# Attention in front of two expert mixtures, one core: tail scores cut into two parts of 288 keys, one exponential, one scaling and two casts placed elsewhere, and another order of work at the end of attention

## The chip, the cores and the metric

One core of a Trainium2 chip runs the whole program in one launch. The metric is the device time of a run in microseconds; 1092.76 us is the median of three runs of the kernel before. TensorE (PE in the rows, PEld its weight loads), VectorE (DVE), ScalarE (ACT), GpSimd (POOL) and SyncE (SP, which issues the transfers here) each work through their own list of instructions in order and wait for each other by semaphores.

## The reference

Sizes: 4 batches, 8 heads, 576 positions, 64 per head; both mixtures have 2304 tokens of 512, 8 experts and 1024 hidden units.

```python
scores = where(causal, -1e9, (q @ k.T) / sqrt(64))      # 576 x 576 for each batch and head
a      = exp(scores - scores.max(-1)); a /= a.sum(-1) + 1e-9
local  = a @ v
mem    = (phi(q) @ M_prev) / (phi(q) @ z_prev + 1e-6)   # phi(x) = elu(x) + 1
x      = g * mem + (1 - g) * local                      # g = sigmoid(beta), by head
# first mixture, soft slots: logits = x @ phi; d = softmax over all tokens; slot_in = d.T @ x
#   two layers per expert on its 4 slots; c = softmax over slots; x = c @ slot_out
# second mixture: P = exp(x @ w_gate - max), 8 rounds of row and column balancing
#   out = sum_e P[:, e] * (relu(x @ w1[e]) @ w2[e])
```

## The kernel before

Attention goes by pairs of heads: 16 pairs, four for each batch. A pair has five steps of queries: steps 0 to 3 are 128 queries each, for both heads, with 128 to 512 keys (in the rows a step is known by its width: step 2 has 384 keys, step 3 has 512); step 4 is the tail, the last 64 queries of both heads on 128 partitions with all 576 keys. A step goes through these stations, and the names are those of the rows:

- `scores`: TensorE multiplies into a PSUM bank `ps` (L385 and L386; the tail L366 and L371, in a bank of 512 keys and one of 64). VectorE negates, scales, masks and takes each row's minimum in one instruction, from `ps` to `sm` (L387, the tail L377 into `smt`); each is followed by a short read of the minimum, `mn`. ScalarE makes the exponentials in place with their sums (L394, `exp`).
- `transposes`: TensorE turns the 128x128 blocks of `sm` into `pt` (L437, the tail L419 and L425), ScalarE or VectorE copies them to `pA` (steps 0 and 1) or `pB` (L62, L66).
- `attend`: once a pair, values times probabilities into `po` (L476), copied to `ot` by ScalarE.
- The steps `post_...` of a pair run during the next pair: `post_r` makes the scale `r` from the sums (L522 to L532), `post_x` turns `ot` back into `px` (L541) and scales it (L544), `post_add` adds the memory part `x` on GpSimd, `post_t` turns `x` into `xT` (L566, copied by L66), `post_logits` multiplies by the slot weights into `pl` (L579, L585) and adds to `lt` (L592).
- The steps `pre_...` prepare a pair two ahead: each of `q` and `k` is split into a rounded part (`qh`, `kh`, and for the tail `qz`, `qx`) and a rest (by GpSimd, L268). `qx` is two copies of 64x64 by ScalarE. `pre_phi` makes phi(q) on VectorE (L336).

After each batch the pair that follows carries the routing of that batch (`route_turn` to `route_slots`: `plt`, `dd`, `pu`, `uacc`), spread over its steps and those of the pair behind it, so two pairs of each of the last three batches have more to do. After the last pair nothing runs beside its post and route steps; then `slot_inputs` (`psl`, `sT`) opens the first mixture, whose first layer is `ph` (L890).

The order of ScalarE and SyncE within attention is the order of the code; TensorE, VectorE and GpSimd get theirs from a scheduler, save where `tc.keep_in_program_order` pins an instruction. The code's order is `scores` of the next step, `attend`, `transposes`, with the steps in between hung at places by a table (`POS`, `at`). `LATE` puts an exponential off: `(2, 1): 1` says that the exponentials of step 2, second head, are issued behind the transposes of step 1, and so behind the copy of `pA`.

Weights of the first mixture come in 32 pieces of 1 MB (`wm`, L99). 14 have room of their own and are loaded during attention; 8 use memory that attention frees at its end; 10 use the memory of the first pieces again and wait until `ph` has read those. Behind them in SyncE's list stand the first weights of the second mixture (`raw`, `w`).

Of the kernel before, what the change touches and what calls it, by code (L numbers as in the profile page):

```python
# [21 lines left out]
def infini_attention_soft_moe_sinkhorn_moe(  # L22
# [22 lines left out]
    P = 128  # L45
# [66 lines left out]
    with ExitStack() as actx:  # L112
# [18 lines left out]
        nc.vector.memset(zero, 0.0)  # L131
        maskt = e2.tile([P, TAIL], BF16, name="maskt")
        nc.gpsimd.memset(maskt, 0.0)
        for j in range(2):
            sl = maskt[64 * j : 64 * j + 64]
            nc.gpsimd.affine_select(
                out=sl, in_=sl, compare_op=ALU.is_ge,
                fill=-BIG, base=0, pattern=[[-1, TAIL]], channel_multiplier=1,
            )
# [150 lines left out]
        def pre_qz(X):  # L290
            n = 4 * P
            qz, qx = X.qt = qtail[X.p % QTB]
            i = nc.vector.tensor_copy(
                qz.rearrange("p (a w) -> p a w", a=3)[:, 0::2], X.qd[:, :, n:]
            )
            if X.p > 1:
                tc.keep_in_program_order(i)
            for h in range(2):
                sl, cl = slice(D * h, D * h + D), slice(TAIL * h, TAIL * h + TAIL)
                copy(CFG["e_qx"], qx[sl, cl], X.qd[sl, h, n:])  # L300
            for h in range(2):
# [43 lines left out]

        LATE = {(0, 0): 4, (0, 1): 4, (1, 1): 0, (2, 1): 1, (3, 0): 2, (3, 1): 2}

# [6 lines left out]
        def scores(X, i):  # L354
            last = i == NT - 1
            n = P * (i + 1) if not last else S
            for h in range(1 if last else 2):
                sm = smt if last else e2.tile([P, 4 * P], F32, tag="sm", name="sm", bufs=SMB)
                mnc = X.mn[:, i, h : h + 1]
                if last:  # L360
                    parts = ((0, 4 * P), (4 * P, S))
                    pss = [pst("ps") for _ in range(2)]
# [11 lines left out]
                    mn2 = X.mn[:, NT, 0:1]  # L374
                    for c, msk in ((0, zero.to_broadcast([P, 4 * P])), (1, maskt)):
                        c0, c1 = parts[c]
                        nc.vector.tensor_tensor_reduce(  # L377
                            out=sm[:, c0:c1], in0=pss[c][:, 0 : c1 - c0], in1=msk, scale=QS,
                            scalar=mn2 if c else 3.0e38, op0=ALU.add, op1=ALU.min,
                            accum_out=mnc if c else mn2,  # L380
                        )
# [81 lines left out]
        def attend(X, i):  # L463
# [4 lines left out]
            for n, w, o0 in ((2, 2 * P, 0), (NT, W2, 2 * P)):  # L468
                po = pst("po")
                for j in range(n):  # L470

                    c0 = P * j if n == 2 else P * max(0, j - 2)
                    for h in range(2):
# [60 lines left out]
        def post_x(X, parts):  # L534
            x1 = X.ot.rearrange("p (t c) -> p t c", t=NT)
            end = X.p == NP - 1
            for t0, t1 in parts:
                px = pst("px")
                nt = t1 - t0
                for t in range(t0, t1):  # L540
                    nc.tensor.transpose(  # L541
                        px[:, P * (t - t0) : P * (t - t0) + P], X.ot[:, P * t : P * t + P], ident
                    )
                nc.vector.tensor_tensor(  # L544
                    out=x1[:, t0:t1].rearrange("p t (h d) -> p (t h) d", h=2),
# [4 lines left out]
                )  # L550
                if end:
                    nc.vector.tensor_add(X.x[:, t0:t1], X.x[:, t0:t1], x1[:, t0:t1])

# [21 lines left out]
        def post_logits(X):  # L575

            pl = pst("pl")
            for t in range(4):
                nc.tensor.matmul(  # L579
                    pl[32 * t : 32 * t + 32, 0:P], phi_sb[:, X.hp],  # L580
                    X.xT[:, P * t : P * t + P], start=True, stop=True,
                )

            for t in range(4):
                nc.tensor.matmul(  # L585
                    pl[32 * t : 32 * t + 32, P : P + TAIL], phi_sb[:, X.hp],
                    X.xT[:, 4 * P : S], start=True, stop=True,
                )
            if X.hp == 0:
                nc.vector.tensor_copy(lt, pl[:, 0 : P + TAIL])  # L590
            else:
                nc.vector.tensor_tensor(  # L592
                    out=lt, in0=lt, in1=pl[:, 0 : P + TAIL], op=ALU.add
                )

        def route_logits(b):
            m5 = e4.tile([P, 1], F32, tag="m5", name="m5")
            nc.vector.tensor_reduce(out=m5, in_=lt, op=ALU.max, axis=AX.X)
            R.m5 = m5

# [75 lines left out]
        def route_slots(b):  # L676
# [7 lines left out]
            for r in range(NHP + 1):  # L684
                for g in range(4):
# [35 lines left out]
        def at(p, n, f, *args):  # L721
# [12 lines left out]
        ROUTE = (  # L734
            ("ra", route_logits), ("rb", route_turn), ("rc", route_max), ("rd", route_factor),
            ("re", route_slots),
        )
        for p in range(NP):
# [18 lines left out]
            for n, (nm, f, *a) in enumerate(MEM):  # L757
                at(p, POS[nm] if p + 1 < NP else POS["mz"] + 2 * n, f, pairs[p], *a)
            if hp == NHP - 1 and p + 1 < NP:
# [4 lines left out]
            else:  # L764
                for n, f, *a in (
                    (1, post_r), (2, post_x, ((0, 2),)), (3, post_t, ((0, 2),)),
                    (3, post_x, ((2, 5),)), (3, post_t, ((2, 5),)), (9, post_logits),
                ):
                    at(p + 1, n, f, pairs[p], *a)
# [960 lines left out]
```

## Time and profile before

| what | value |
|---|---|
| median of three runs | 1092.76 us (1092.0 to 1095.72) |
| the profiled execution | 1093.55 us, its span 1091.8 us |
| TensorE busy over the span | 1058.1 us, 97% |
| VectorE, ScalarE, GpSimd busy | 790.7, 623.0, 730.1 us |
| attention with its end | from 0 to 254.75 us |
| first mixture | 254.75 to about 294 us |
| second mixture | the rest, where the page has TensorE at 9 tenths in all slices |

A busy share is that of an engine's instructions in the span. A wait is given in square brackets or behind the releaser. The granted clock of TensorE is 1.00 for 2.4 GHz and 0.50 for 1.2 GHz.

### The profile page before, as it was taken

To read this page: it belongs to the slowest core of one execution; us is meant where nothing else is said; L and a number is where in the kernel's file an instruction comes from. 1 tells how busy PE (TensorE), PEld (TensorE's weight loads), DVE (VectorE), ACT (ScalarE), POOL (GpSimd) and SP (SyncE) were. 2 spreads that over 40 slices of the span, in tenths; PEclk is the share of its full clock that TensorE was granted. 3 is DMA by queue.
4 is the path that set the end of the run, shared out by engine and by line. 5 is a ranking of instruction groups with operands and counts; after the bars stand their busy time and mean duration, and the time that the engine had idled before them with its cause. 6 is when DMAs were issued, how large, how long until landed. Compare 5 with 4: busy or idle time off the path is not lost.

```text
span 1091.8 us, 24586 instructions
## 1 busy us (share of the span) xinstructions
PE 1058.1 (97%) x9157; PEld 968.1 (89%) x9157; DVE 790.7 (72%) x1764; ACT 623.0 (57%) x1322; POOL 730.1 (67%) x683
## 2 busy tenths in 40 slices
PE   6999999988999999999999999999999999999998
PEld 4878878764477899999999999999999999999998
DVE  7888878764157466777777777777777777877776
ACT  7998989841243666456445645554564464456442
POOL 6655646400153499679678867968886796889765
PEclk9999999997989999999999999999999999999999
DMA  9476767568812014113210421321042132110211
GB/s 212 135 216 188 215 202 217 155 235 356 351 55 87 1 20 159 36 20 118 65 24 11 156 39 21 114 67 24 12 155 40 21 113 65 24 16 15 69 54 59
DMA packets 103574, 113.08 MB, mean 104 GB/s; under 512 B 69152, under 2 KB 79520, under 8 KB 99360
## 3 DMA queue, kind: packets, MB, share of 16 engines
q1 hardware_dynamic: 103024, 111.42, 33.8%
q8 instruction: 73, 1.20, 0.5%
q14 instruction: 45, 0.37, 0.1%
q10 hardware_dynamic: 432, 0.09, 0.0%
HBM read 95.74 MB, written 4.72 MB: 92 GB/s over the span
## 4 chain that ended last, share of the span: by engine, by line
PE 80%; DVE 5%; DMA 5%; ACT 4%; issue 3%; POOL 3%; SPq 0%; DVEq 0%; ACTq 0%; POOLq 0%
PE y L1530 56%; PE l L1146 5%; PE po L476 3%; PE pt L437 2%; PE y L1493 2%; DMA kd<-in_k_dram 2%; ACT sm L394 2%; PE pa L1093 2%; DMA wm<-in_moe_w_dram 2%; DMA w<-in_moe_w_dram 1%; PE ph L890 1%; PE ps L371 1%; PE ps L366 1%; DVE sm L387 1%; PE pt L419 1%
## 5 line engine op out<-in xcount | busy, mean ns | idle before, releaser
L1170 DVE SCALAR_TENSOR_TENSOR f<-l,f 128x512 f32<-128x512 f32 x268 | 183.8, 686 | 83.9 <-ACT a11h L1176 70.1
L1187 POOL TENSOR_TENSOR s1l<-f,s1h 128x512 fp32r<-128x512 f32 x67 | 87.3, 1303 | 116.6 <-ACT s1h L1176 116.6
L1544 DVE TENSOR_TENSOR accA<-accA,y 128x512 f32<-128x512 f32 x125 | 85.6, 685 | 54.0 <-PE y L1530 54.0
L1166 ACT ACTIVATE f<-l 128x512 f32<-128x512 f32 x67 | 40.1, 598 | 120.1 <-PE l L1146 119.5
L1176 ACT ACTIVATE a12h<-l 128x512 fp32r<-128x512 f32 x72 | 43.3, 601 | 103.0 <-PE y L1530 83.0
L1187 POOL TENSOR_TENSOR s4l<-f,s4h 128x512 fp32r<-128x512 f32 x67 | 87.7, 1308 | 17.3 <-PE y L1530 17.3
L1544 DVE TENSOR_TENSOR accB<-accB,y 128x512 f32<-128x512 f32 x125 | 85.7, 685 | 4.2
L1187 POOL TENSOR_TENSOR s2l<-f,s2h 128x512 fp32r<-128x512 f32 x67 | 87.6, 1307 | 1.3 <-ACT s2h L1176 0.5
L1187 POOL TENSOR_TENSOR s3l<-f,s3h 128x512 fp32r<-128x512 f32 x67 | 87.8, 1311 | 0.0
L1146 PE MATMUL l<-c4T,a 128*128 128x256 f32 x576 | 78.1, 278 | 0.0
L394 ACT ACTIVATE sm<-sm,mn 128x128 f32<-128x128 f32 (+3 forms) x128 | 70.9, 557 | 8.3 <-DVE mn L387 7.9
L1530 PE MATMUL y<-T2h,s2h 128*128 128x256 f32 x268 | 74.7, 279 | 0.0
L1530 PE MATMUL y<-T2l,s2h 128*128 128x256 f32 x268 | 74.1, 276 | 0.0
L1530 PE MATMUL y<-T2h,s2l 128*128 128x256 f32 x268 | 74.1, 276 | 0.0
L1530 PE MATMUL y<-T1h,s1h 128*128 128x256 f32 x268 | 74.0, 276 | 0.0
L1530 PE MATMUL y<-T1l,s1h 128*128 128x256 f32 x268 | 74.0, 276 | 0.0
L1530 PE MATMUL y<-T1h,s1l 128*128 128x256 f32 x268 | 74.0, 276 | 0.0
L1530 PE MATMUL y<-T4h,a22h 128*128 128x256 f32 x268 | 74.0, 276 | 0.0
L1530 PE MATMUL y<-T4l,a22h 128*128 128x256 f32 x268 | 74.0, 276 | 0.0
L1530 PE MATMUL y<-T4h,a22l 128*128 128x256 f32 x268 | 74.0, 276 | 0.0
L1530 PE MATMUL y<-BB1h,s3l 128*128 128x256 f32 x268 | 73.1, 276 | 0.9 <-POOL s3l L1187 0.9
L1530 PE MATMUL y<-BB2h,a12h 128*128 128x256 f32 x268 | 73.6, 279 | 0.0
(324 smaller groups left out, 4063.1 us busy)
## 6 DMA issues: line engine op xcount, KB each, us to landing
wm<-in_moe_w_dram SPq DMA_DIRECT2D x32, 1024.0 KB, 7.2
raw<-in_moe_w_dram SPq DMA_DIRECT2D x32, 512.0 KB, 3.6
w<-in_moe_w_dram SPq DMA_DIRECT2D x32, 512.0 KB, 5.4
qd<-in_q_dram SPq DMA_DIRECT2D x30, 288.0 KB, 4.2
kd<-in_k_dram SPq DMA_DIRECT2D x30, 288.0 KB, 4.3
c4T<-ct SPq DMA_DIRECT2D x224, 32.0 KB, 2.0
qp<-in_q_dram SPq DMA_DIRECT2D x15, 288.0 KB, 3.0
vt<-in_v_dram SPq DMA_DIRECT2D x16, 256.0 KB, 4.5
```

What stands on the lines that cost most here:

```text
L394: nc.scalar.activation(out=sm[:, 0:n], in_=sm[:, 0:n], func=AF.Exp, scale=-1.0, bias=mnc, accum_out=X.sums[:, i, h : h + 1],)
L437: nc.tensor.transpose(pt[:, o_ : o_ + P], pr[:, P * j : P * j + P], ident)
L476: nc.tensor.matmul(po[64 * h : 64 * h + 64, c0:w], X.vt[:, j, h, :], rhs, start=(j == 0), stop=(j == n - 1),)
L1093: nc.tensor.matmul(pa[32 * j : 32 * j + 32, 0:256], soT[:, c, :], w1[j][:, c, :], start=(c == 0), stop=(c == KD - 1),)
L1146: nc.tensor.matmul(ph[:, f, :], a4s[e][:, P * (KH * j + f) : P * (KH * j + f) + P], c4T[:, UT * u : UT * u + UT], start=True, stop=True,)
L1166: nc.scalar.activation(out=f_tile(g, nm), in_=ph(g, nm), func=AF.Relu)
L1170: nc.vector.scalar_tensor_tensor(out=f_tile(g, nm), in0=ph(g, src), scalar=0.0, in1=b, op0=ALU.max, op1=op)
L1176: nc.scalar.activation(out=h_tile(g, nm, "h"), in_=ph(g, nm) if a else FU[g, nm], func=AF.Relu if a else AF.Copy)
L1187: nc.gpsimd.tensor_tensor(out=lo, in0=FU[g, nm], in1=hi, op=ALU.subtract)
L1493: nc.tensor.matmul(Y[g, i], X[g, f"a{i}{j}", "hhl"[n]][:, f, :], BB[j, "hlh"[n]][:, f].rearrange("p a c -> p (a c)"), start=j == 1 and f = ...
L1530: nc.tensor.matmul(o_, a[:, f, :], b[:, f, :], start=n == 0, stop=n == 3 * KH - 1)
L1544: nc.vector.tensor_tensor(out=acc, in0=acc, in1=y, op=ALU.add)
```

## The change

1. The tail's scores go into two banks of 288 keys in place of 512 and 64. The mask tile `maskt` grows from 64 to 288 columns.
2. `(2, 1)` leaves `LATE`: both exponentials of step 2 are issued together, ahead of the copy of `pA`.
3. The scaling of `ot` (`post_x`, the part of four blocks) is kept in program order, which is behind the minima of step 2.
4. The two copies to `qx` go from ScalarE to GpSimd, from the third pair on.
5. The end of the last pair is written anew: `post_r` ahead of `attend`; `end_x`, `end_t` and `end_l` in place of `post_x`, `post_t` and `post_logits`, block by block, where one VectorE instruction for each block and head (64 columns) scales and adds; the first two blocks are turned back while `attend` still runs; copies to `xT` by ScalarE; the last sum of the logits and their maximum in one instruction, in the last pair of each batch; the sums of the weights in `route_slots` ahead of most `pu` in the last batch; the memory steps of the last pair earlier by one to three places.

```diff
-        maskt = e2.tile([P, TAIL], BF16, name="maskt")
+        SH = S // 2
+        maskt = e2.tile([P, SH], BF16, name="maskt")
...
-                copy(CFG["e_qx"], qx[sl, cl], X.qd[sl, h, n:])
+                copy("P" if X.p > 1 else CFG["e_qx"], qx[sl, cl], X.qd[sl, h, n:])
...
-        LATE = {(0, 0): 4, (0, 1): 4, (1, 1): 0, (2, 1): 1, (3, 0): 2, (3, 1): 2}
+        LATE = {(0, 0): 4, (0, 1): 4, (1, 1): 0, (3, 0): 2, (3, 1): 2}
...
-                    parts = ((0, 4 * P), (4 * P, S))
+                    parts = ((0, SH), (SH, S))
...
-                    for c, msk in ((0, zero.to_broadcast([P, 4 * P])), (1, maskt)):
+                    for c, msk in ((0, zero.to_broadcast([P, SH])), (1, maskt)):
...
+                    if n == NT and j == 2 and X.p == NP - 1:
+                        end_x(X, 0, 2)
...
+        def end_x(X, t0, t1):
+            px = pst("px")
+            for t in range(t0, t1):
+                nc.tensor.transpose(
+                    px[:, P * (t - t0) : P * (t - t0) + P], X.ot[:, P * t : P * t + P], ident
+                )
+            for t in range(t0, t1):
+                for h in range(2):
+                    c0 = P * (t - t0) + D * h
+                    xs = X.x[:, t, D * h : D * h + D]
+                    nc.vector.scalar_tensor_tensor(
+                        out=xs, in0=px[:, c0 : c0 + D], scalar=X.r2[:, t, h : h + 1], in1=xs,
+                        op0=ALU.mult, op1=ALU.add,
+                    )
+
+        def end_t(X, t0, t1):
...
+            px = pst("pxT")
+            for t in range(t0, t1):
+                nc.tensor.transpose(px[:, P * (t - t0) : P * (t - t0) + P], X.x[:, t], ident)
+            a, z = P * t0, min(P * t1, S)
+            copy("A", X.xT[:, a:z], px[:, 0 : z - a])
+
+        def end_l(X, t0, t1):
...
-                nc.vector.tensor_tensor(
+                i = nc.vector.tensor_tensor(
                     out=x1[:, t0:t1].rearrange("p t (h d) -> p (t h) d", h=2),
...
-                if end:
-                    nc.vector.tensor_add(X.x[:, t0:t1], X.x[:, t0:t1], x1[:, t0:t1])
+                if t0 == 0:
+                    tc.keep_in_program_order(i)
...
+            elif X.hp == NHP - 1:
+                R.m5 = e4.tile([P, 1], F32, tag="m5", name="m5")
+                nc.vector.tensor_tensor_reduce(
+                    out=lt, in0=lt, in1=pl[:, 0 : P + TAIL], scale=1.0, scalar=-3.0e38,
+                    op0=ALU.add, op1=ALU.max, accum_out=R.m5,
+                )
...
-        def route_logits(b):
-            m5 = e4.tile([P, 1], F32, tag="m5", name="m5")
-            nc.vector.tensor_reduce(out=m5, in_=lt, op=ALU.max, axis=AX.X)
-            R.m5 = m5
...
-                if r == 3:
+                if r == (0 if b == B - 1 else 3):
                     weight_sums(b)
...
-                at(p, POS[nm] if p + 1 < NP else POS["mz"] + 2 * n, f, pairs[p], *a)
+                at(p, POS[nm] if p + 1 < NP else (11, 13, 14, 14)[n], f, pairs[p], *a)
...
-                    (1, post_r), (2, post_x, ((0, 2),)), (3, post_t, ((0, 2),)),
-                    (3, post_x, ((2, 5),)), (3, post_t, ((2, 5),)), (9, post_logits),
+                    (0, post_r), (1, end_t, 0, 2), (1, end_x, 2, 5), (2, end_l, 0, 2),
+                    (2, end_t, 2, 4), (2, end_t, 4, 5), (3, end_l, 2, 4), (3, end_l, 4, 5),
+                    (9, post_logits),
```

The order on VectorE in an ordinary pair, from the scale `r` to the minima of step 3, before:

```order
L387 ISA sm,mn<-ps,maskw 128x384
L387 ISA mn 128x1
L532 RECIPROCAL r_858<-r_858 128x10
L544 TENSOR_TENSOR ot<-px,r_858 128x512
L387 ISA sm,mn<-ps,maskw 128x384
L387 ISA mn 128x1
L544 TENSOR_TENSOR ot<-px,r_858 128x128
L387 ISA sm,mn<-ps,maskw 128x512
```

and in the change:

```order
L388 ISA sm,mn<-ps,maskw 128x384
L388 ISA mn 128x1
L574 RECIPROCAL r_858<-r_858 128x10
L585 TENSOR_TENSOR ot<-px,r_858 128x128
L388 ISA sm,mn<-ps,maskw 128x384
L388 ISA mn 128x1
L585 TENSOR_TENSOR ot<-px,r_858 128x512
L388 ISA sm,mn<-ps,maskw 128x512
```

The scalings of 512 and of 128 columns have changed places, so the small one, not the large one, now stands between the two minima of step 2. ScalarE at the same place of a pair, before:

```order
L394 ACTIVATE sm,sums<-sm,mn 128x256
L394 ACTIVATE sm,sums<-sm,mn 128x384
L62 ACTIVATE pA<-pt 128x2x256
L394 ACTIVATE sm,sums<-sm,mn 128x384
L62 ACTIVATE pB<-pt 128x3x128
L394 ACTIVATE sm,sums<-sm,mn 128x512 x2
L62 ACTIVATE pB<-pt 128x3x128
L62 ACTIVATE qh<-qd 128x1024
L394 ACTIVATE smt,sums<-smt,mn 128x576
L62 ACTIVATE qx_148<-qd 64x64 x2
L62 ACTIVATE kh<-kd 128x1152
```

and in the change:

```order
L395 ACTIVATE sm,sums<-sm,mn 128x256
L395 ACTIVATE sm,sums<-sm,mn 128x384 x2
L62 ACTIVATE pA<-pt 128x2x256
L62 ACTIVATE pB<-pt 128x3x128
L395 ACTIVATE sm,sums<-sm,mn 128x512 x2
L62 ACTIVATE pB<-pt 128x3x128
L62 ACTIVATE qh<-qd 128x1024
L395 ACTIVATE smt,sums<-smt,mn 128x576
L62 ACTIVATE kh<-kd 128x1152
```

The copy of `pA` has gone behind the second exponential of step 2, and the two copies to `qx` have left the list. TensorE at the end of the last pair, from the end of `attend` to the turning of the logits, before:

```order
L476 MATMUL po<-pB,vt 64x64 x2
L522 MATMUL pz<-sums,ident 64x1
L541 MATMUL px<-ident,ot 128x128 x2
L566 MATMUL pxT<-ident,x 128x128 x2
L541 MATMUL px<-ident,ot 128x128 x3
L566 MATMUL pxT<-ident,x 128x128 x3
L579 MATMUL pl<-xT,phi_sb 32x128 x4
L585 MATMUL pl<-xT,phi_sb 32x64 x4
L604 MATMUL plt<-ident,lt 128x128
```

and in the change:

```order
L477 MATMUL po<-pB,vt 64x64 x2
L507 MATMUL pxT<-ident,x 128x128
L489 MATMUL px<-ident,ot 128x128 x2
L507 MATMUL pxT<-ident,x 128x128
L489 MATMUL px<-ident,ot 128x128
L514 MATMUL pl<-xT,phi_sb 32x128 x2
L507 MATMUL pxT<-ident,x 128x128 x3
L514 MATMUL pl<-xT,phi_sb 32x128 x2
L520 MATMUL pl<-xT,phi_sb 32x64 x4
L637 MATMUL plt<-ident,lt 128x128
```

The scale's `pz` and the first two `px` now stand ahead of these rows, among those of `po`.

## Rows read from the trace of the kernel before

**Rows 1.** Windows: us; busy of PE, PEld, DVE, ACT, POOL; granted clock; DMA share; GB/s.

```profile
100.97:114.25 13.28, 12.86 (x119) 10.92 (x116) 10.94 (x41) 12.32 (x33) 7.88 (x10) 1.00 0.59 182
127.55:142.83 15.28, 14.32 (x124) 11.56 (x122) 12.19 (x49) 12.77 (x36) 7.89 (x10) 1.00 0.77 225
142.83:158.12 15.29, 14.41 (x166) 12.15 (x167) 12.03 (x44) 12.53 (x34) 7.88 (x10) 1.00 0.60 179
```

**Rows 2.** Timeline of a pair: start, us, engine, instruction, [idle before <-releaser].

```profile
113.00 0.69 DVE L544 TENSOR_TENSOR ot<-px,r 128x512 f32<-128x512 f32 x1
...
113.60 0.55 DVE L387 CUSTOM_DVE_ANT_0 sm<-ps,maskw 128x384 f32<-128x384 f32 x1
...
114.08 0.28 DVE L544 TENSOR_TENSOR ot<-px,r 128x128 f32<-128x128 f32 x1
114.25 0.61 ACT L394 ACTIVATE sm<-sm,mn 128x384 f32<-128x384 f32 x1 [0.29 <-DVE mn L387]
114.28 0.68 DVE L387 CUSTOM_DVE_ANT_0 sm<-ps,maskw 128x512 f32<-128x512 f32 x1
...
115.01 0.55 PE L437 MATMUL pt<-ident,sm 128*128 128x128 f32 x3 [0.51 <-ACT sm L394]
...
118.04 0.71 POOL L268 TENSOR_TENSOR qz<-qd,qz 64x64 fp32r<-64x64 f32 x2 [1.77 <-DVE r L501]
...
118.73 0.51 ACT L62 ACTIVATE qx<-qd 64x64 fp32r<-64x64 f32 x2
```

**Rows 3.** Chain that ended last, the same pair: start, us, what; then step 2's scores.

```profile
115.56 0.47 PE ps L366 x2
116.03 0.46 PE ps L371 x2
116.49 0.14 PE ps L366 x2
116.63 0.23 PE ps L371 x2
...
155.69 0.17 PE ps L386
```

**Rows 4.** Timelines of GpSimd and VectorE around phi(q), three pairs.

```profile
25.50 2.90 POOL L268 TENSOR_TENSOR klz<-kd,kh 64x576 fp32r<-64x576 f32 x2
...
27.47 1.55 DVE L336 SCALAR_TENSOR_TENSOR qp<-qe,qp 128x576 f32<-128x576 f32 x1 [1.90 <-ACT qp L331]
...
121.52 2.88 POOL L268 TENSOR_TENSOR klz<-kd,kh 64x576 fp32r<-64x576 f32 x2
...
123.89 1.13 DVE L336 SCALAR_TENSOR_TENSOR qp<-qe,qp 128x576 f32<-128x576 f32 x1 [0.94 <-ACT qp L331]
...
224.93 0.76 DVE L336 SCALAR_TENSOR_TENSOR qp<-qe,qp 128x576 f32<-128x576 f32 x1 [1.19 <-ACT qp L331]
```

**Rows 5.** Chain that ended last: a load at the start, then the end of attention.

```profile
14.51 8.90 DMA kd<-in_k_dram
...
244.31 0.47 PE plt L604
...
250.43 0.51 PE pu L687 x6
...
254.75 9.63 PE ph L890 x64
```

**Rows 6.** Timeline at the same end: the copy of `ot`, the wait ahead of `psl`.

```profile
237.94 0.44 ACT L62 ACTIVATE ot<-po 128x320 f32<-128x320 f32 x1 [1.61 <-PE pz L522]
...
252.48 1.89 PE L707 MATMUL psl<-stkr,uacc 128*128 128x32 f32 x8 [1.42 <-DVE stkr L674]
```

**Rows 7.** Windows behind attention (columns as rows 1); SyncE's waits from 200 to 300.

```profile
254.00:256.00 2.00, 1.62 (x10) 0.63 (x14) 1.52 (x8) 0.34 (x1) 0.00 (x0) 0.50 0.16 61
256.00:258.00 2.00, 2.00 (x12) 0.39 (x8) 1.97 (x11) 0.34 (x1) 0.00 (x0) 0.50 0.44 61
...
SPq L99 <- PE ph L890: 18.3, 10, 11.2
```

More of the change, by code (lines that the diff above doesn't have):

```diff
@@ L131, in infini_attention_soft_moe_sinkhorn_moe @@
         nc.vector.memset(zero, 0.0)
-        maskt = e2.tile([P, TAIL], BF16, name="maskt")
+        SH = S // 2
+        maskt = e2.tile([P, SH], BF16, name="maskt")
         nc.gpsimd.memset(maskt, 0.0)
         for j in range(2):
-            sl = maskt[64 * j : 64 * j + 64]
+            sl = maskt[64 * j : 64 * j + 64, SH - TAIL :]
             nc.gpsimd.affine_select(
@@ L479, in attend @@
                         )
+                    if n == NT and j == 2 and X.p == NP - 1:
+                        end_x(X, 0, 2)
                 copy(CFG["e_oA" if n == 2 else "e_oB"], X.ot[:, o0 : o0 + w], po[:, 0:w])
+        def end_x(X, t0, t1):
[14 more added lines that the diff above has]
+            if t0 == 0:
+                X.xT = e5.tile([P, S], F32, tag="sc", name="xT")
+                X.pl = pst("pl")
+            px = pst("pxT")
[4 more added lines that the diff above has]
+        def end_l(X, t0, t1):
+            for t in range(t0, t1):
+                if t < 4:
+                    nc.tensor.matmul(
+                        X.pl[32 * t : 32 * t + 32, 0:P], phi_sb[:, X.hp],
+                        X.xT[:, P * t : P * t + P], start=True, stop=True,
+                    )
+                    continue
+                for j in range(4):
+                    nc.tensor.matmul(
+                        X.pl[32 * j : 32 * j + 32, P : P + TAIL], phi_sb[:, X.hp],
+                        X.xT[:, 4 * P : S], start=True, stop=True,
+                    )
         def post_mem(X):
@@ L535, in post_x @@
             x1 = X.ot.rearrange("p (t c) -> p t c", t=NT)
-            end = X.p == NP - 1
             for t0, t1 in parts:
@@ L550, in post_x @@
                 )
-                if end:
-                    nc.vector.tensor_add(X.x[:, t0:t1], X.x[:, t0:t1], x1[:, t0:t1])
+                if t0 == 0:
+                    tc.keep_in_program_order(i)
         def post_add(X):
@@ L575, in post_logits @@
         def post_logits(X):
[L577 to L588, printed above, removed]
+            if X.p < NP - 1:
+                X.pl = pst("pl")
+                end_l(X, 0, NT)
+            pl = X.pl
             if X.hp == 0:
                 nc.vector.tensor_copy(lt, pl[:, 0 : P + TAIL])
+            elif X.hp == NHP - 1:
[3 more added lines that the diff above has]
+                    op0=ALU.add, op1=ALU.max, accum_out=R.m5,
+                )
             else:
@@ L734, in infini_attention_soft_moe_sinkhorn_moe @@
         ROUTE = (
-            ("ra", route_logits), ("rb", route_turn), ("rc", route_max), ("rd", route_factor),
+            ("rb", route_turn), ("rc", route_max), ("rd", route_factor),
             ("re", route_slots),
```

## The prediction

> **What bounds the kernel now.** I read the windows by pair first, then one pair's timeline and chain, then the end of attention. A window of [rows 1] starts where the second exponential of step 2 starts (E below), so its length is a pair's period. An ordinary pair takes 13.28 us and TensorE is busy in 12.86 of them; ScalarE has 12.32, VectorE 10.94, GpSimd 7.88. TensorE sets the pace and idles 0.42. The two pairs with routing take 15.28 and 15.29, and TensorE idles 0.96 and 0.88 in them. So in attention a gain can come only from less work of TensorE, or from its waits, and the waits are small.
>
> The one wait of an ordinary pair is in [rows 2]: TensorE stands 0.51 before it turns step 2, second head (115.01), until the exponential of 114.25 is done; that stood 0.29 for its minimum, and the minimum began only at 113.60, behind the scaling of 512 columns that VectorE took up at 113.00.
>
> Behind attention the picture changes. From 237.94 [rows 6] to 254.75, where `ph` starts [rows 5], one small operation waits for another. SyncE waits for `ph` ten times, 18.3 us together [rows 7]: the ten last pieces of the first mixture's weights follow the first `ph`. The transfers stand nearly still before that: their share is 0.16 in 254 to 256 and 0.44 in 256 to 258 [rows 7], 1.68 + 1.12 = 2.8 us idle. From there the first mixture goes at the pace of its weights, and what starts `ph` earlier moves the rest of the program.
>
> **Tail in two parts of 288.** Same columns, eight matmuls as before. In the chain they take 0.47 + 0.46 + 0.14 + 0.23 = 1.30 us [rows 3]. A matmul of 512 takes 0.233, one of 64 takes 0.092 on average (0.07 and 0.115), one of 384 takes 0.17 [rows 3]. For 288, in proportion to 384 and 512, I take 0.132: 8 x 0.132 = 1.06, 0.24 less. Bounds: not below the 0.115 of a narrow one (0.92, 0.38 less); not above the straight line between 64 and 512, 0.163 (1.30, nothing). The minima on VectorE have the same columns and start after half of the scores; VectorE has 2.3 us spare in a pair [rows 1], so I count nothing. The wider mask is made once at the start.
>
> **Scaling behind the minima, exponentials joined.** From the scaling of 512 to the next instruction VectorE needs 113.60 - 113.00 = 0.60; from that of 128, 114.28 - 114.08 = 0.20 [rows 2]. The small one now stands ahead of the minimum, so minimum and exponential come 0.40 earlier, and of the wait of 0.42 to 0.51 some 0.1 stays. The large scaling moves to where the small one was; GpSimd's addition needs both and is no later. On ScalarE the exponential no longer queues behind the copy of `pA`. It now blocks the copy in turn: `pA` is wanted by `attend` of the next pair, and ScalarE, at 12.32 less 0.51 for `qx` [rows 1, 2], has 11.8 us of work in a period of 12.6.
>
> **`qx` on GpSimd.** ScalarE loses 0.51 a pair [rows 2], off TensorE's path. GpSimd gets two casts of 64x64; it has no such row, the nearest are its two subtractions of that size, 0.71 together [rows 2]. What stands behind them on GpSimd: `qz`, `qh`, `klz`. They matter through a second chain. In [rows 4], `klz` ends at 121.52 + 2.88 = 124.40 and VectorE's phi(q), begun at 123.89, ends at 125.02: 0.62 later. In an earlier pair 25.50 + 2.90 = 28.40 and 27.47 + 1.55 = 29.02: again 0.62. Where GpSimd is idle it takes 0.76 (224.93). So phi(q) ends 0.62 after `klz`, and the minima of steps 1 and 2 stand behind it. The Trainium skill says the same (SBUF — State Buffer, "Who interferes with whom"): a VectorE instruction with two SBUF inputs and a GpSimd instruction that reads SBUF exclude each other for the whole instruction. The trace agrees, 0.62 both times; by that rule alone anything added ahead of `klz` could be paid for in full.
>
> Worked out from E = 114.25: GpSimd's train starts with `qz` at 118.04, E + 3.79, after a wait of 1.77, and runs through to 124.40, E + 10.15, so 6.36 us; phi ends at E + 10.77, and the next E (127.55, E + 13.30) comes 2.53 later, now 2.13. In the changed kernel the casts may start when the tail's scores are done: E + 2.61 before (116.63 + 0.23), E + 2.37 with the shorter tail. With 0.71 for both, they end at E + 3.1, inside the old wait. With `qz` between E + 3.2 and E + 3.8, the next E comes 6.36 + 0.62 + 2.13 later: E + 12.3 to E + 12.9. TensorE alone would allow 13.30 - 0.24 - 0.51 = 12.55. I take 12.65: 0.65 gained in an ordinary pair. Bounds 0.40 (only one of the two terms) and 0.85 (the lower bound of 288, and the whole wait).
>
> **Pairs with routing.** 0.24 for the tail, and of 0.92 us idle (mean of the two) the part that falls away: `pu` and its wait go behind the second head's turning, and the scaling of the sums behind the copies that `pl` waits for. I take 0.66 of it, 0.25 stays: 0.9 a pair, between 0.5 and 1.16.
>
> **Attention together.** Of 16 pairs, six carry routing: 6 x 0.9 = 5.4. Eight are ordinary: 8 x 0.65 = 5.2. The first pair waits for loads until 23.4 (14.51 + 8.90 [rows 5]); what it gains is hidden there. For the rest of the start, and for the last pair, whose `attend` now has `pz` and two `px` in it (about 0.25), I take 0.5, between 0 and 1.2. Sum 11.1.
>
> **The fused end.** Before, from the copy of `ot` (237.94 [rows 6]) to `plt` (244.31 [rows 5]) are 6.37 us, in two rounds of turn, scale, add, turn, copy. Now the first two blocks are done beside `attend`. What is left in series: copy of `ot` 0.44 [rows 6]; two turnings 0.3; six VectorE instructions of 64 columns at 0.20, the step of the 128-column scaling [rows 2], 1.2; turning and copy 0.8; `pl` 0.5; logits with their maximum 0.4; seven hand-overs of 0.05: 4.0, so 2.3 less (1.8 with 0.28 each, that row's whole duration). Behind `pu` (ends 250.43 + 0.51 = 250.94 [rows 5]) `psl` starts at 252.48, after a wait of 1.42 [rows 6], the last link being the scale of the sums; that is now made beside `pu`, which leaves two half additions: about 0.7 less. Less the 0.25 by which `attend` ends later, `ph` starts 2.75 earlier. But only 2.8 us of idle transfer time lie ahead of the ten pieces [rows 7], and the eight before them start behind the longer `attend`: 2.8 - 0.25 = 2.55 is the most. I take 2.5, between 0 and 2.8. The granted clock is 0.50 there [rows 7], the lower level, after TensorE had been idle in most of the end; I count it as unchanged.
>
> **Sum.** 11.1 + 2.5 = 13.6. The profiled execution took 1093.55 (span 1091.8): 1079.95. It lies 0.8 above the median of the three runs, so 1079.2 against 1092.76. Bounds: least 8 x 0.40 + 6 x 0.5 + 0 + 0 = 6.2, 1086.6; most 6.8 + 7.0 + 1.2 + 2.8 = 17.8, 1075.0.
>
> **Rivals.**
> - *GpSimd's chain becomes the pair's bound.* Casts of 0.7 each put `qz` at E + 3.8 and the next E at 12.95: 0.3 less gain in 14 pairs, 1083.4. For it: phi always ends 0.62 behind `klz`. Against it: GpSimd's 1.77 us of waiting.
> - *The end gives nothing*, since the first weights still on their way fill the gap, or ten small instructions cost as much as four large: 1081.7.
> - *The wait moves.* The shorter tail saves nothing and TensorE waits next for another engine: only routing at 0.5, the start, and the end remain, 3.0 + 0.3 + 2.5 = 5.8: 1087.0. For it: ScalarE is only 0.54 below TensorE in [rows 1].
> - *No effect in time*, the first mixture's weights being what is waited for anyway: 1092.8. Against it: those weights wait for `ph` [rows 7].
> - *Slower:* the casts are slow on GpSimd. The pair gets longer than 13.30 once `qz` starts after E + 4.19, when two casts take over 1.8 us, 0.9 each. At half of `klz`'s pair, 1.44 each [rows 4], `qz` starts at E + 5.25 and the period is 14.36, 1.06 longer: 14 x 1.06 - 2.5 = 12.3 more, 1105.
>
> **How the numbers follow.** Forecast 0.53, GpSimd 0.15, end 0.15, wait moved 0.10, no effect 0.04, slower 0.03. Three runs spread over 0.3% (3.3 us), about what tells a difference from none. Faster by more: the first four, 0.93; within: 0.04; slower: 0.03. The range reaches from the most that the terms allow, 1075, to the third rival, 1087.
>
> **What would show it.** In windows from E to E: ordinary periods near 12.65 with TensorE's idle time at 0.1 or less, routing ones near 14.4. The tail's eight matmuls in about 1.06. The exponential's start 0.4 earlier relative to the scaling. `qz` on GpSimd at most 3.8 behind E. `plt` about 4.1 behind the copy of `ot`, `psl` 0.8 behind `pu`, and no gap in the transfers ahead of `ph`. From `ph` to the end all as before. Wrong would make it: casts over 0.9 us, a new wait ahead of `pl` or `pt`, or a second mixture that moved by another amount than `ph`.

## The result

The changed kernel takes 1077.76 us, the median of four runs (1076.01 to 1080.93), against 1092.38 (1089.92 to 1095.72) for the kernel before: ratio 0.9873, 95% interval 0.9847 to 0.9900, 14.6 us less by the medians. The profiled execution took 1077.04 us (span 1075.3, 16.5 less than before). One run of the last kernel in the table of experiments (1103.6 us) was in a slower state of the chip and is left out of its median.

By stations of the two traces (E1 to E15: the starts of the second exponential of step 2 in 15 consecutive pairs; `y`: the first matmul of the second mixture's second layer):

| stretch | before | changed | gained | forecast |
|---|---|---|---|---|
| up to E1 | 31.03 | 30.30 | 0.73 | 0.5 (with the last pair) |
| E1 to E15 | 197.65 | 187.58 | 10.07 | 10.6 |
| of it eight ordinary pairs | 106.63 | 101.49 | 5.14 | 5.2 |
| of it six pairs with routing | 91.02 | 86.09 | 4.93 | 5.4 |
| E15 to `ph` | 26.07 | 23.19 | 2.88 | 2.5 |
| `ph` to first `y` | 49.97 | 47.74 | 2.23 | 0 |
| first `y` to the end | 787.1 | 786.5 | 0.6 | 0 |

The windows that answer to [rows 1] (an ordinary pair, then the two pairs with the second batch's routing):

```profile
96.10:108.77 12.67, 12.64 (x117) 10.74 (x116) 11.15 (x41) 11.82 (x31) 8.36 (x12) 1.00 0.74 226
121.83:135.63 13.80, 13.71 (x121) 11.27 (x120) 11.62 (x44) 11.82 (x32) 8.37 (x12) 1.00 0.77 230
135.63:150.93 15.30, 15.17 (x169) 12.42 (x168) 13.30 (x49) 12.41 (x33) 8.41 (x12) 1.00 0.55 166
```

TensorE is busy in 12.64 of 12.67 us. From E to E the first routing pair gained 1.39 (15.19 before), the second 0.08 (15.38 before; the border of 142.83 in [rows 1] lies 0.09 behind E). The share of each depends on the station: the change moves E against TensorE's work, and from the first `pma` of a pair to that of the next the same two gain 0.43 and 1.04 (16.71 and 13.87 before, 16.28 and 12.83 now). Together they gain 1.47. The pair's own timeline, against [rows 2, 4]:

```profile
95.24 0.29 DVE L585 TENSOR_TENSOR ot<-px,r 128x128 f32<-128x128 f32 x1 [0.24 <-PE px L582]
95.45 0.55 DVE L388 CUSTOM_DVE_ANT_0 sm<-ps,maskw 128x384 f32<-128x384 f32 x1
95.92 0.69 DVE L585 TENSOR_TENSOR ot<-px,r 128x512 f32<-128x512 f32 x1
96.10 0.62 ACT L395 ACTIVATE sm<-sm,mn 128x384 f32<-128x384 f32 x1 [0.48 <-DVE mn L388]
96.35 1.06 PE L438 MATMUL pt<-ident,sm 128*128 128x128 f32 x6
...
98.54 0.53 POOL L64 CAST qx<-qd 64x64 fp32r<-64x64 f32 x2
99.34 0.71 POOL L269 TENSOR_TENSOR qz<-qd,qz 64x64 fp32r<-64x64 f32 x2 [0.28 <-DVE r L543]
...
100.55 2.60 POOL L269 TENSOR_TENSOR qh<-qd,qh 64x512 fp32r<-64x512 f32 x2 [0.40 <-ACT qh L62]
...
103.12 2.90 POOL L269 TENSOR_TENSOR klz<-kd,kh 64x576 fp32r<-64x576 f32 x2
...
105.29 1.34 DVE L337 SCALAR_TENSOR_TENSOR qp<-qe,qp 128x576 f32<-128x576 f32 x1 [0.73 <-ACT qp L332]
```

The small scaling stands ahead of the minimum (0.21 from one to the other, 0.60 before), and the six turnings of step 2 now follow each other. The two casts take 0.53 on GpSimd, `qz` starts 3.24 behind E (bound in the forecast: 3.8), GpSimd then waits 0.40 for ScalarE's `qh`, `klz` ends 9.92 behind E, phi(q) 0.61 later, the next E 2.14 after that: 12.67 in all, as long as TensorE's busy time. In the chain the tail is four pairs of matmuls (against [rows 3]), 1.07 us:

```profile
97.41 0.27 PE ps L367 x2
97.68 0.27 PE ps L372 x2
97.95 0.26 PE ps L367 x2
98.21 0.26 PE ps L372 x2
```

The end of attention in the chain, against [rows 5, 6], then two windows and SyncE's wait against [rows 7]:

```profile
227.64 0.45 ACT ot L62
...
231.57 0.33 PE plt L637
...
237.32 0.67 PE pu L720 x7
...
238.80 1.90 PE psl L740 x8
...
241.07 8.50 PE ph L924 x64
```

```profile
228.00:230.00 2.00, 1.51 (x10) 0.84 (x10) 1.18 (x6) 0.46 (x2) 0.00 (x0) 1.00 0.64 172
240.00:242.00 2.00, 1.62 (x12) 0.83 (x15) 1.11 (x5) 0.57 (x2) 0.00 (x0) 0.50 0.99 406
242.00:244.00 2.00, 2.00 (x16) 0.52 (x12) 2.00 (x11) 0.00 (x0) 0.00 (x0) 0.50 0.99 418
244.00:246.00 2.00, 2.00 (x24) 0.52 (x20) 1.91 (x9) 0.34 (x1) 0.00 (x0) 1.00 0.74 262
```

```profile
SPq L99 <- PE ph L924: 16.4, 10, 10.5
```

From the start of the copy of `ot` to `plt` are 3.93 us (6.37 before), from the end of `pu` (237.99) to `psl` 0.81 (1.54). The transfers no longer stand still ahead of `ph`: their share is 0.99 up to 244.

### The profile page after: what moved, and what is told of

Same layout as the page of the kernel before. It is cut to its first block, busy times and chain, and to the rows that moved or that the text cites. A ratio compares the mean times of both kernels' runs of the same rounds, so it can differ in the third digit from the quotient of the medians.

```text
span 1075.3 us, 24580 instructions
## 1 busy us (share of the span) xinstructions
PE 1050.6 (98%) x9157; PEld 963.0 (90%) x9157; DVE 789.2 (73%) x1768; ACT 615.5 (57%) x1297; POOL 738.4 (69%) x711
## 4 chain that ended last, share of the span: by engine, by line
PE 84%; issue 4%; POOL 4%; ACT 3%; DVE 2%; DMA 2%; SPq 0%; ACTq 0%; DVEq 0%; POOLq 0%
PE y L1564 57%; PE l L1180 5%; PE po L477 3%; PE pt L438 3%; DMA kd<-in_k_dram 2%; PE ph L924 1%; PE pso L946 1%; PE pa L1127 1%; PE ps L386 1%; PE ps L387 1%; PE pma L531 1%; PE y L1527 1%; ACT sm L395 1%; PE ps L367 1%; PE ps L372 1%
```

## The experiments

Before, changed and the twelve kernels of the experiments in one table, with the stations of each one's profile. An ordinary pair is the median of the eight. The kernel before was run again beside each series (medians 1091.17 to 1093.39 us); a ratio is to those runs, so it is the safer comparison than two medians of different series.

| kernel | median us | ratio to before, 95% | ordinary pair | E1 to E15 | E15 to `ph` | E15 to `y` |
|---|---|---|---|---|---|---|
| before | 1092.38 | | 13.29 | 197.65 | 26.07 | 76.04 |
| changed | 1077.76 | 0.9873 (0.9847 to 0.9900) | 12.67 | 187.58 | 23.19 | 70.93 |
| changed, tail undone | 1084.75 | 0.9921 (0.9894 to 0.9947) | 12.81 | 192.38 | 23.00 | 68.86 |
| changed, joining undone | 1085.88 | 0.9919 (0.9892 to 0.9947) | 12.89 | 193.01 | 23.02 | 70.71 |
| changed, `qx` undone | 1084.91 | 0.9917 (0.9888 to 0.9947) | 13.10 | 191.40 | 23.41 | 69.79 |
| changed, end undone | 1079.75 | 0.9873 (0.9840 to 0.9906) | 12.69 | 187.37 | 25.48 | 71.35 |
| before, tail alone | 1085.80 | 0.9949 (0.9925 to 0.9973) | 13.01 | 193.36 | 25.28 | 70.87 |
| before, joining alone | 1088.49 | 0.9965 (0.9947 to 0.9983) | 13.09 | 193.68 | 26.07 | 72.37 |
| before, `qx` alone | 1089.88 | 0.9982 (0.9961 to 1.0003) | 13.20 | 197.59 | 25.76 | 73.00 |
| before, end alone | 1090.63 | 0.9984 (0.9964 to 1.0004) | 13.30 | 197.72 | 23.60 | 69.87 |
| changed, `qx` on ScalarE far back | 1089.70 | 0.9981 (0.9962 to 1.0000) | 13.27 | 198.71 | 23.18 | 71.09 |
| changed, `qx` on ScalarE behind `pB` | 1080.47 | 0.9899 (0.9870 to 0.9928) | 12.56 | 186.74 | 23.41 | 70.11 |
| changed, three times the casts | 1081.50 | 0.9911 (0.9890 to 0.9932) | 13.21 | 191.89 | 22.53 | 69.65 |
| changed, sums in their own bank | 1077.99 | 0.9881 (0.9856 to 0.9905) | 12.68 | 187.04 | 23.18 | 69.97 |

The ratios are uncertain by some 0.3% (3 us); the stations mostly agree better between profiles of one order of work, and the readings below rest on them. Single pairs can differ: the ordinary pair ahead of the second batch's routing took 13.06 in the changed kernel and 12.69 with the end undone, so a difference of 0.4 in E1 to E15 says little.

### Taking one part out of the change

Tail:

```diff
-        SH = S // 2
-        maskt = e2.tile([P, SH], BF16, name="maskt")
+        SH = 4 * P
+        maskt = e2.tile([P, TAIL], BF16, name="maskt")
...
```

> The changed kernel with the tail's scores back in banks of 512 and 64 keys. Theory (TensorE's own work sets the pair): its eight matmuls go from 1.06 back to 1.30 us, an ordinary pair from 12.67 to about 12.9, some 15 pairs by 0.24: 3.6 us more, 1081.4. Rival (GpSimd's train and phi(q) set the pair, TensorE's saved work only became idle time): periods stay at 12.67, TensorE's idle time in a pair falls from what it has, time within 1 us of 1077.8.

Measured: ordinary pairs 12.81, between the two theories, and 1084.75 us. The other 0.1 was room that TensorE had in the changed kernel: the run with `qx` behind `pB`, below, has pairs of 12.54, and 12.54 + 0.24 = 12.78. The pairs with routing lost more than ordinary ones: 89.73 us for the six against 86.09.

Joining:

```diff
-        LATE = {(0, 0): 4, (0, 1): 4, (1, 1): 0, (3, 0): 2, (3, 1): 2}
+        LATE = {(0, 0): 4, (0, 1): 4, (1, 1): 0, (2, 1): 1, (3, 0): 2, (3, 1): 2}
...
-                if t0 == 0:
-                    tc.keep_in_program_order(i)
```

> The changed kernel with the second exponential of step 2 put off again behind the copy of pA, and the scaling of 512 columns no longer pinned behind the minima. Theory: TensorE's wait ahead of step 2, second head, is back at 0.4 to 0.5 us, ordinary pairs at 13.0 to 13.1, 14 pairs by 0.36 to 0.45: 5 to 6.3 us more, 1083 to 1084. Rival (the chain over klz and phi(q) sets the pair and hides that wait): under 1.5 us more.

Measured: 12.89, 1085.88 us. The rival falls; the theory's 13.0 to 13.1 was 0.15 too long. The order of the exponentials and the pinned scaling were only undone together, here and below; which of them gives how much was not tested.

The casts `qx`:

```diff
-                copy("P" if X.p > 1 else CFG["e_qx"], qx[sl, cl], X.qd[sl, h, n:])
+                copy(CFG["e_qx"], qx[sl, cl], X.qd[sl, h, n:])
```

> The changed kernel with the two casts qx back on ScalarE. Theory: they are off the path on either engine, ScalarE's 12.3 us still fit into a pair of 12.67; periods as now, time within 1 us of 1077.8. Rival (ScalarE has no room left): kh on ScalarE comes 0.51 later, klz, phi(q) and the next minima with it, up to 0.5 in each of 14 pairs, 1081 to 1085.

Measured: 13.10 in six of the eight ordinary pairs, 1084.91 us. (The first took 12.63 and the last 12.49, in the changed kernel 12.62 and 12.49.) My theory falls: on ScalarE the casts cost 0.43 of each of the six. The timeline of one of them says how:

```profile
101.54 0.52 ACT L62 ACTIVATE qx<-qd 64x64 fp32r<-64x64 f32 x2
...
102.08 1.17 ACT L62 ACTIVATE kh<-kd 128x1152 fp32r<-128x1152 f32 x1
...
103.16 0.80 ACT L62 ACTIVATE pB<-pt 128x128 f32<-128x128 f32 x3
...
103.47 0.19 PEld L386 LDWEIGHTS ps<-kh,qh 128*128 128x128 f32 x1 [0.65 <-ACT pB L62]
```

TensorE is held at the scores of step 1 until ScalarE has copied the last block of step 3's `pt`, first head, to `pB` (the first of the three copies, done at 103.42). The scores read nothing of `pB`; what the copy gives them is the PSUM bank, which is taken in turn from one pool of eight. The rival's time came, 1081 to 1085, but not by its way: phi(q) ends at 107.13, 2.55 ahead of the next E, and needs 2.14. From E (96.58) ScalarE works without a gap up to that copy, 6.89 us, and TensorE needs 6.21 from there to the next E (109.68): 13.10. Without the 0.52 of `qx` that way would be 12.58, just below the 12.67 of the changed kernel. And the kernel before was close to the same limit. Its rows from E = 100.97:

```profile
107.05 0.27 ACT L62 ACTIVATE pB<-pt 128x128 f32<-128x128 f32 x1
107.50 0.36 PE L385 MATMUL ps<-kh,qh 128*128 128x256 f32 x1
```

The copy was done at E + 6.35, TensorE came at E + 6.53: 0.18 of room, less than the 0.64 that the tail and the joining were to bring.

The end:

```diff
-                    (0, post_r), (1, end_t, 0, 2), (1, end_x, 2, 5), (2, end_l, 0, 2),
-                    (2, end_t, 2, 4), (2, end_t, 4, 5), (3, end_l, 2, 4), (3, end_l, 4, 5),
-                    (9, post_logits),
+                    (1, post_r), (2, post_x, ((0, 2),)), (3, post_t, ((0, 2),)),
+                    (3, post_x, ((2, 5),)), (3, post_t, ((2, 5),)), (9, post_logits),
...
-                if r == (0 if b == B - 1 else 3):
+                if r == 3:
...
```

> The changed kernel with the end of the last pair as before (scale, add and turn in two rounds, logits and maximum apart, sums of the weights late, memory steps late). Theory: plt again 6.4 behind the copy of ot, psl 1.5 behind pu, ph 2.9 us later against the last ordinary pair, and all behind it later by as much: 1080.3 to 1081. Rival 1 (the end's gain is swallowed by the transfers): 1077.8. Rival 2 (the 2.8 us that the changed kernel gained behind ph, where TensorE's granted clock was 1.00 in place of 0.50 while the second mixture starts, also hang on the end): 1083 to 1084, with the clock at 0.50 again behind pa.

Measured: `ph` 2.29 later behind E15, but the first `y` only 0.42, and 1079.75 us, with the same ratio as the change. The clock behind `pa` was 1.00 here too, so rival 2 falls. This pair of profiles alone would say that the end gives nothing; it is taken up again below.

### One part alone

The same edits, made to the kernel before.

> The kernel before with both exponentials of step 2 together and the scaling of 512 columns behind the minima, nothing else. Theory: TensorE's own way would allow 13.29 - 0.40 = 12.89, but ScalarE's way by qx, kh and the copy of pB, which now starts 0.4 earlier and carries the copy of pA as well, holds the pair at 13.1: ordinary pairs 13.1, TensorE waiting for the copy of pB, 2 to 3 us less than before. Rival (edits add up): 12.9, 5 to 6 us less.

Measured: 13.09, E1 to E15 3.97 shorter, ratio 0.9965. The new theory holds: half of the wait that the joining removes comes back as a wait for the copy of `pB`, as the timeline of an ordinary pair shows (and its window below it):

```profile
108.07 0.19 PEld L386 LDWEIGHTS ps<-kh,qh 128*128 128x128 f32 x1 [0.34 <-ACT pB L62]
```

```profile
101.20:114.29 13.09, 12.97 (x116) 10.82 (x115) 11.01 (x41) 12.19 (x33) 7.87 (x10) 1.00 0.63 193
```

TensorE's matmuls count as busy for 12.97 us here, against 12.86 for the same work before [rows 1], in a shorter pair: part of the wait lies within the modelled busy time, and the busy share alone would have hidden it.

> The kernel before with the two casts qx on GpSimd and nothing else. Theory (in the kernel before TensorE waits only for the late exponential of step 2, and ScalarE's way by kh and pB has room): ordinary pairs stay at 13.2 to 13.3, TensorE's wait ahead of step 2 stays at 0.4 to 0.5, time within 1.5 us of the kernel before. Rival (ScalarE's order sets the pair there too): ordinary pairs at 12.9, 5 to 6 us less.

Measured: 13.20, E1 to E15 unchanged (0.06), ratio 0.9982. TensorE still waits 0.42 for the exponential, as its timeline shows:

```profile
102.65 0.55 PE L437 MATMUL pt<-ident,sm 128*128 128x128 f32 x3 [0.42 <-ACT sm L394]
```

The casts give 0.09 alone and 0.43 on top of the two other parts.

> The kernel before with the tail's scores in two banks of 288 keys and nothing else. Theory (TensorE's own way sets the pair): ordinary pairs 13.29 - 0.24 = 13.05, some 15 pairs, 3 to 3.5 us less than before. Rival (the wait for step 2's exponential takes up what the tail saves): 13.2 to 13.3, under 1 us.

Measured: 13.01, 0.28 less than before, E1 to E15 4.29 shorter, ratio 0.9949; TensorE's wait ahead of step 2 stays at 0.43. The theory holds.

> The kernel before with the new end of the last pair and nothing else. Theory 1 (my forecast: what starts ph earlier moves all behind it): ph 2.3 to 2.9 earlier against the last ordinary pair, the first y of the second mixture too, 2 to 3 us less than before. Theory 2 (the eight pieces that wait for attention's memory set the pace up to pa, and they come no earlier): ph 2.3 to 2.9 earlier, the bulk of pa and the first y at most 0.5 earlier, no change in time. For the 3 us that the changed kernel gained between pa and y at a higher granted clock: if they hang on the end they appear here, if on chance they may or may not.

Measured: `ph` 23.60 behind E15 (26.07 before), first `y` 69.87 (76.04), ratio 0.9984 with an interval that holds both none and 3.9 us. The time does not decide between the theories, nor does one profile.

### Where `qx` stands on ScalarE

Both kernels leave `qx` on ScalarE, at another place; `pre_qx` makes the two copies that stood in `pre_qz`. The first issues it behind phi(q)'s exponential:

```diff
-                copy("P" if X.p > 1 else CFG["e_qx"], qx[sl, cl], X.qd[sl, h, n:])
...
+            if p < NP - 2:
+                at(p, 14, pre_qx, pairs[p + 2])
```

> The changed kernel with qx on ScalarE again, but issued behind the copies of pB and phi(q)'s exponential, no longer ahead of kh. Theory (with qx ahead of them, kh and the copy of pB come 0.52 later, and TensorE waits 0.65 for the bank that this copy frees): that wait goes, ordinary pairs are back from 13.10 to 12.7 with ScalarE's work unchanged at 12.3, time within 1.5 us of 1077.8. Rival (ScalarE's sum of work is what is too much): periods stay at 13.1, 1083 to 1085.

Measured: 13.1 to 15.1 in six of the eight ordinary pairs (12.61 in the first, 12.48 in the last), 1089.7 us. TensorE no longer waits for `pB`, but a new wait came in, so that the run tells nothing of the dispute: `qx` reads `qd`, and the load of the next `qd` waits for it at the head of SyncE's list; `qp` behind it comes late. SyncE's waits from 40 to 90 (us in total, times, longest), then the timeline of a pair of that stretch:

```profile
SPq L208 <- ACT qx L62: 27.5, 4, 8.4
```

```profile
67.57 0.68 ACT L335 ACTIVATE qe<-qp 128x576 f32<-128x576 f32 x1 [1.51 <-DMA qp<-in_q_dram]
...
70.33 0.90 PE L586 MATMUL px<-ident,ot 128*128 128x128 f32 x4 [1.67 <-ACT ot L62]
```

The second puts it directly behind the copies of `pB`:

```diff
                 transposes(pairs[steps[g][0]], steps[g][1])
+                if steps[g][1] == NT - 1 and steps[g][0] < NP - 2:
+                    pre_qx(pairs[steps[g][0] + 2])
```

> The changed kernel with qx on ScalarE once more, now directly behind the tail's copies of pB, where the buffer qd comes free about when GpSimd's qh would free it anyway (the run before put qx 2 us further back, and the loads behind qd came late). Theory (only the place of qx ahead of kh and pB matters): ordinary pairs 12.7, at most 12.9, no wait of TensorE for the copy of pB, time within 2 us of 1077.8. Rival (ScalarE's 0.52 costs wherever it stands): 13.1, 1083 to 1085.

Measured: ordinary pairs 12.56, E1 to E15 186.74, even 0.84 shorter than in the changed kernel (0.52 of it in the pair that took 13.06 there); 1080.47 us, a ratio that the interval does not part from the change's. A pair's window and its timeline:

```profile
97.05:109.68 12.63, 12.61 (x117) 10.66 (x115) 10.33 (x40) 11.91 (x34) 7.91 (x10) 1.00 0.79 230
```

```profile
103.05 1.05 ACT L62 ACTIVATE pB<-pt 128x128 f32<-128x128 f32 x3
...
103.37 0.39 PE L390 MATMUL ps<-kh,qh 128*128 128x256 f32 x1
...
103.98 0.51 ACT L62 ACTIVATE qx<-qd 64x64 fp32r<-64x64 f32 x2
...
107.67 0.75 DVE L341 SCALAR_TENSOR_TENSOR qp<-qe,qp 128x576 f32<-128x576 f32 x1
```

The same 0.51 us on the same engine costs nothing once it is behind the copy that frees the bank. So it is the place, not ScalarE's sum of work. In this kernel phi(q) also comes only after `klz` has ended (106.98) and takes 0.75, so that the second chain no longer sets the pair. TensorE's own way is then at most 12.54 (three of these pairs), near the 12.55 of the forecast; the 12.64 that it counts as busy in the changed kernel hold some waiting.

### Three times the casts on GpSimd

```diff
-                copy("P" if X.p > 1 else CFG["e_qx"], qx[sl, cl], X.qd[sl, h, n:])
+                for _ in range(3 if X.p > 1 else 1):
+                    copy("P" if X.p > 1 else CFG["e_qx"], qx[sl, cl], X.qd[sl, h, n:])
```

> The changed kernel with each of the two casts qx made three times on GpSimd (the same values again): 1.06 us more work ahead of qz in each pair. Theory (GpSimd's train to klz, phi(q) 0.61 behind it, then the minima up to the next E 2.14 later are a chain as long as the pair): 0.40 of it goes into GpSimd's wait for qh, 0.66 is paid, ordinary pairs 13.3, 8 to 9 us more than 1077.8. Rival (only TensorE bounds the pair): 12.7 to 12.8, no more than 1 us.

Measured: ordinary pairs 13.21, 0.53 longer, E1 to E15 4.31 longer, 1081.5 us. The chain is real; its price was 0.13 smaller, since GpSimd's 0.28 wait ahead of `qz` takes up a part too, and the pairs with routing pay less (87.12 against 86.09, 0.17 each), so that the time rose by 4, not by 8 or 9.

```profile
99.47 1.69 POOL L64 CAST qx<-qd 64x64 fp32r<-64x64 f32 x6
...
104.58 2.90 POOL L269 TENSOR_TENSOR klz<-kd,kh 64x576 fp32r<-64x576 f32 x2
...
106.22 1.88 DVE L338 SCALAR_TENSOR_TENSOR qp<-qe,qp 128x576 f32<-128x576 f32 x1 [0.20 <-ACT qp L333]
```

In this timeline `klz` ends at 107.48, phi(q) at 108.10, 0.62 later, the next E at 110.23, 2.13 after that. Phi(q) took 0.75 with `klz` done, 1.34 in the changed kernel and 1.88 here, and ended 0.61 to 0.62 behind `klz` in the last two. The Trainium skill (SBUF — State Buffer, "Who interferes with whom") has the two exclude each other; these rows agree.

### A version with the sums of the weights in a bank of their own

```diff
-            pd = R.pb[:, 65:66]
+            pd = (R.pb if b in (0, B - 1) else pst("pd"))[:, 65:66]
```

> The changed kernel with the sums of the weights of the second and third batch in a PSUM bank of their own, so that TensorE's order has them among pu and no longer in the middle of the tail. Theory (the second routing pair of these batches lost in front what it gained behind, since the sums wait for the factor's copy and break the tail into 1.59 in place of 1.06 us): those two pairs 15.30 down to 14.7 or 14.8, 1.0 to 1.2 us in all, 1076.7. Rival (the work only changes place): 15.3.

Measured: the two pairs 14.93 and 14.95 in place of 15.30, one first routing pair 14.35 in place of 13.80, E1 to E15 0.54 shorter; 1077.99 us, which can't be told from the change. In the third batch the sums cost 0.35: its first routing pair is as long as it was. In the second batch it is not shown: there the first pair lost 0.55, so that the two are 0.17 longer together, and 0.20 shorter with the ordinary pair ahead of them (12.69 in place of 13.06). So the theory has the direction, and half of the 1.0 to 1.2 that it forecast. In the changed kernel the sums stand in the middle of the tail, which takes from 138.73 to 140.32, 1.59 us (timeline of the changed kernel):

```profile
139.11 0.29 PE L372 MATMUL ps<-klz,qx 128*128 128x288 f32 x1
139.33 0.24 PE L687 MATMUL pb<-ones,dd 128*32 128x1 f32 x8
139.42 0.20 PE L690 MATMUL pb<-ones,dd 128*32 128x1 f32 x2
139.55 0.40 PE L372 MATMUL ps<-klz,qx 128*128 128x288 f32 x1
```

## Why the prediction was right, and where it was wrong

**Time and sum.** 1079.2 was forecast, with 13.6 us of gain; the medians differ by 14.6, with 10.9 to 16.7 by the interval. Sum and range held, but one step behind them was wrong: the move of `qx` was put at nothing. Without it the ordinary pairs would have gained 0.19, not the 0.65 of the forecast, so it is luck that the change had that move in it and that the sum came right. (A small slip beside it: the three runs of before span 3.7 us, 1092.0 to 1095.72, not 3.3.)

**Tail.** 1.07 us for the eight, 1.06 as worked out from 384 and 512 columns. Alone it gives 0.28 a pair, forecast 0.24.

**Joining.** Counted at 0.40 a pair whatever else is done. Alone it gave 0.20, on top of the others 0.22.

**`qx`, the step that failed:** "ScalarE loses 0.51 a pair [rows 2], off TensorE's path." I read it off the busy time, 12.32 against 12.86 [rows 1]. But ScalarE's way from E to the copy of `pB` has no gap, and TensorE needs the bank. Without the move, tail and joining together give 13.10, a gain of 0.19 out of 0.64 (the third rival, "the wait moves", and its reason); with it 12.67: the step was put at nothing and is worth 0.43 a pair. The ordinary pairs by parts: none 13.29; tail 13.01; joining 13.09; `qx` 13.20; tail and joining 13.10; tail and `qx` 12.89; joining and `qx` 12.81; all 12.67. The gains do not add up because three ways of nearly the same length close the pair: TensorE's work (at most 12.54, from the run with `qx` behind `pB`), ScalarE up to the bank and TensorE behind it (12.58, from the run with `qx` undone), and ScalarE's `qh` with GpSimd's train and phi(q) behind it (12.67). Each part shortens another one.

**GpSimd's chain.** Right in mechanism: `qz` at E + 3.24, 0.61 and 2.14 at its end, and added work is paid in the ordinary pairs. By the forecast's own terms this `qz` gives a pair of 3.24 + 6.36 + 0.62 + 2.13 = 12.35, and it took 12.67: the train from `qz` to the end of `klz` was 6.68, since GpSimd waits 0.40 within it for ScalarE's `qh`, a wait that the forecast did not have. The chain is now the longest of the three ways, by 0.1; the rival's 12.95 needed casts of 0.7 each, and the two together took 0.53.

**Routing.** 0.82 a pair, forecast 0.9, but from E to E not evenly: 1.4 and 0.1 in the second and in the third batch, 0.24 and 1.74 in the first. In part that is E's doing, as said with the result. That "`pu` and its wait go behind the second head's turning" is so in the trace; the order of the sums took 0.35 back in one batch. Why the rest of the forecast did not come is open.

**Start and last pair.** E1 came 0.73 earlier, but over these profiles it lies anywhere from 29.07 to 31.86, so nothing is shown there.

**End.** The two parts were right: 3.93 (forecast 4.0) and 0.81 (0.8). Which of the rewritten steps gives how much was not tested apart. ("TensorE had been idle in most of the end" holds only ahead of the fall of the clock, 2.04 us busy of the 4.90 up to 242.8; from there to `ph` it is busy in 8.05 of 11.95.) `ph` comes 2.88 earlier, and over all profiles, nine with the new end and five with the old, 23.17 against 25.73 behind E15, 2.56. Of this the first `y` keeps 1.8: 70.11 against 71.90, the mean of the four old ones without the profile of before. Single profiles scatter by some 1 us around both (from `ph` to the bulk of `pa` they take 37.9 to 40.2), enough for the 0.42 of the pair with the end undone. In that stretch weights are waited for: in the chain of before 264.40 to 293.87 is transfers, but for 0.1 us. The times do not show the end by themselves.

**"From `ph` to the end all as before"** failed in this pair of profiles, by a stretch that the change doesn't touch. From the bulk of `pa` to the first `y`, timeline and window, before and then after:

```profile
293.91 3.60 PE L1093 MATMUL pa<-w,soT 128*32 128x256 f32 x26 [0.51 <-DMA w<-in_moe_w_dram]
```

```profile
293.91:304.72 10.81, 10.34 (x69) 7.64 (x69) 2.23 (x8) 3.93 (x11) 4.02 (x4) 0.66 0.55 206
```

```profile
281.11 1.91 PE L1127 MATMUL pa<-w,soT 128*32 128x256 f32 x26 [0.66 <-DMA w<-in_moe_w_dram]
```

```profile
281.11:288.81 7.70, 7.12 (x70) 5.84 (x70) 2.24 (x8) 2.58 (x6) 2.06 (x2) 1.00 0.71 245
```

Before, the granted clock was at its lower level (0.50) in 10.2 of the 13.6 us from 294.0 to 307.6, after short waits of TensorE from 291.6 on (0.39, 0.32, 0.51); the changed kernel waited there for 0.39, 0.32, 0.65 and 0.66 and stayed at 1.00. The 26 matmuls of `pa` took 3.60 in place of 1.91. In the other thirteen profiles, four with the old end among them, that way to the first `y` is 7.69 to 7.72 us: the 3.1 us belong to that one execution. (A fall of the clock as such is not: three of the thirteen have 3.4 us at 0.50 that begin 0.2 to 0.4 ahead of the first `y`.) The weights had taken 0.9 of the earlier `ph` back by then (39.16 from `ph` to the bulk of `pa` before, 40.04 after), so 2.23 are left. What repeats over the profiles is 10.07 from E1 to E15 (10.35 between the two kernels with the other end, 197.72 and 187.37) and 1.8 of the end, together 11.9 us of the 14.6 between the medians.

## What to carry to other kernels

An engine is off the path only if its own list, followed from the event that starts the period up to the last thing it hands to the bounding engine (a freed bank counts), leaves room; its sum of busy time doesn't tell. Where several such ways are nearly equal, a part that gives nothing alone can carry the gain of the others, so each is tried both alone and left out. And a read that is moved back on one engine holds the buffer that it reads, and with it every load that stands behind in the queue.

## What the runs showed of the hardware beyond this

The matmuls of the second mixture ran at two paces at a granted clock of 1.00, with TensorE busy throughout. Two stretches of 20 us, in the changed kernel and in the one with `qx` behind `pB`:

```profile
429.00:449.00 20.00, 20.00 (x179) 20.00 (x178) 15.84 (x28) 10.57 (x20) 15.78 (x13) 1.00 0.12 27
```

```profile
428.00:448.00 20.00, 20.00 (x172) 20.00 (x171) 15.19 (x27) 10.83 (x20) 13.87 (x12) 1.00 0.14 31
```

179 matmuls against 172, 4% fewer; in the 160 us that begin 80 behind the first `y` the counts are 1435 and 1393, and three of the fourteen profiles have the lower number there. Seven more have the slower pace in shorter stretches: four in a first part of the 160 (1424 or 1425), and four in the last 80 us of the program (172 in 20 us; one profile has both). The four without such a stretch are the shortest. From the first `y` to the end are 786.3 to 794.1 us over the fourteen profiles: 786.3 to 787.2 in those four, 791.1, 792.1 and 794.1 in the three. The cause is open; it is a good part of why single times of one kernel spread by several us.
